# Backward value products on block-diagonal weights, new instruction orders, and other queues in the last stage

## The chip, the cores and the metric

One NeuronCore of a Trainium2 chip runs the whole program as one launch. Its five instruction streams are TensorE (PE in the profile; PEld is its weight loads), VectorE (DVE), ScalarE (ACT), GpSimd (POOL) and SyncE (SP), which only issues transfers; ScalarE and GpSimd issue transfers too. The metric is the device time of the launch in microseconds. Before the change six runs gave 3076.02 to 3081.55 us, median 3080.12 us.

## What is computed

The program computes the output and all ten gradients of `x + A(layernorm(x)) + B(layernorm(x))`. B is an MLP with a squared ReLU (512 to 1792 to 512). A is an attention over 64 segments of 32 rows, with 32 heads of 128 and 8 memory rows which each segment takes from the output of the one before, so the segments run one after the other:

```python
for s in range(n_seg):                       # 64
    xs = x[:, s * seg_len:(s + 1) * seg_len, :].copy()   # 32 rows
    h = jnp.concatenate([mem, xs], axis=1)   # 8 + 32 rows
    q = jnp.einsum('btd,dhe->bhte', h, Wq)
    k = jnp.einsum('btd,dhe->bhte', h, Wk)
    v = jnp.einsum('btd,dhe->bhte', h, Wv)
    scores = jnp.einsum('bhqe,bhke->bhqk', q, k) * scale
    scores = jnp.where(mask[None, None], scores, -1000000000.0)
    p = _softmax(scores, axis=-1)
    o = jnp.einsum('bhqk,bhke->bhqe', p, v)
    o = jnp.einsum('bhte,hed->btd', o, Wo)
    mem = o[:, :M, :].copy()
    outs.append(o[:, M:, :])
```

Inputs and outputs are bf16; the sequence has 2048 rows of width 512. The backward goes through the segments from the last to the first. In it, the gradient of v is the product of the transposed softmax weights with the gradient of the attention's output (the "value product"), one 32x128 head at a time, 32 heads a segment.

## The kernel before

*Stages*, by their place in the profiled execution: the MLP, the layernorm and first loads up to about 300 us; 64 forward steps, about 304 to 1185; the backward of left rows and the MLP's weight gradients, to 1455; 64 backward steps, 1455 to 2445; the last stage, the weight gradients of Wq, Wk, Wv, Wo and the gradient of x, to 3079.5.

*Rows and left rows.* A step's 40 rows are held as 32 that it works on in turn (8 memory rows and the segment's last 24) and the segment's first eight, its "left rows". Four steps form a block; the left rows of a block (4 x 8) are projected and have their gradients multiplied by the weights together, in operations named `L.*`. 32 heads lie as four head groups (`HG`, on 32 partitions each) of eight heads (`KH`).

*The order.* Each stage of steps is written out by hand: `F_ORDER` and `B_ORDER` are four strings each, one for each place of a step in its block, and `play` goes through the names in them and issues each operation. A `-` or `+` behind a name takes the operation from an earlier or later step (or block), so work of neighbouring steps is interleaved. The strings set the order of every engine's queue. `ENGS` says for each PSUM-to-SBUF copy whether ScalarE (helper line L372) or VectorE (L375) does it.

*A backward step* in the names of `B_ORDER`:

- `o0mm`, `o1mm` (L390): the output gradient's rows times Wo; `o*ev` copies them to `gON`; `o*fl` (L163) flips them through TensorE, and `o*te` copies the flips to `gOT`.
- `vp0`, `vp1`: the value products of heads 0-3 and 4-7 of each head group, by `outer` (L545). For each head, `outer` issues a matmul of a 32-row group: weights `gON[32g:32g+32, 128 columns]`, right side `P` (32x40), then one of the left rows (weights `b_gOL`, right side `b_PG`, 16 columns), into a PSUM round of two tiles (`b_pp`). Four head groups run on four row groups of the array. `vea`, `veb` copy heads' rows out, `vla`, `vlb` the left part (`b_gvL`).
- `s0`, `s1` (L435), `d1*` to `d4*`, `tu*`: the gradient of the scores, of which `gS` and `gST` come.
- `kp*`, `qp*`: the same kind of outer products for k and q, with evacuations `ke*`, `kl*`, `qe*`.
- `vg*`, `kg*`, `qg*` (L458): the products with Wv, Wk, Wq, gathered into one PSUM tile; `ra`, `rb` copy it, `ta`, `tb` (L467) transpose it, `HT` and `xt` (L480) reduce over the head groups. `HT` hands the 8 memory rows to the step that follows.
- `ldp`, `ldq`, `ldn` (L1216 to L1219) load P, q and k rows of a step, on GpSimd's queue; `ldk` and `vtr` use SyncE's. `vc` (L1229, L1230) builds `b_vT` on GpSimd from the transposed v rows (`b_vl`) and from `b_vTL`, the left rows, which `ldt` loads by a DMA transpose, once a block.
- For a block, `L.tr`-operations (`qtr`, `ktr`, `vtr`, L1171) transpose the left gradients by DMA into `gNat`, `*st` (L1173) store them, `L.xt` sums the left rows into the first 8 columns of `b_XT`, and `L.sx` stores it to `S_XG`. `ldv` loads `b_PG` and `b_gOL`.

*The last stage* (`slot_side`, `rows_of`, `loads`, `input_rows`, `leave`, and the loop that follows): sixteen columns of weight gradients, each eight products of 20 matmuls of 128x512. `slot_side` loads the two sides, `GOc` (of `S_GM`) and `HNc` (of `S_HT`), by 16 DMA transposes of 512 columns and four plain loads each, on SyncE's queue. `rows_of` loads the other side of each column, `gn`: for Wo by plain loads (the first column's on ScalarE's queue, others on SyncE's), for the others by 16 DMA transposes (L1387). Three buffers of it turn, and column i issues the load for i + 2. The first column's eight products run row block by row block at once, over eight PSUM tiles; each later column runs one product after the other. `leave` copies a product to `wt` on ScalarE (L1437) and stores it from the same queue (L1438). `input_rows` makes the gradient of x for one block of rows after each column (TensorE transposes at L1418, the rest on VectorE, ScalarE and GpSimd, its transfers on GpSimd's queue).

Of the kernel before, what the change touches and what calls it, by code (L numbers as in the profile page):

```python
# [26 lines left out]
def kernel(  # L27
# [114 lines left out]
    S_XG = dram.tile([NB, P, DC, P], F32, name="S_XG")  # L142

# [327 lines left out]
    def left_sums(XT, T):  # L471

        for c in range(DC):
            nc.vector.tensor_reduce(XT[:, c, :, 0:M], T[:, c * P:(c + 1) * P].rearrange("p (g j t) -> p j t g", g=HG, j=SPB),
                                    axis=AX.X, op=ALU.add)
# [103 lines left out]
    def play(order, n, steps, lefts, step, blk, done=None):  # L579
# [22 lines left out]
        "L.oa0 HT",  # L602
        "k0mm xt- q1mm k0ev q1ev q0mm L.oa1 q0ev k1mm L.out- q0fl k0fl q1fl k1ev L.mst- k1fl q0Te kl k0Te k1Te s0 "
        "q1Te L.X0 s1 mx0 sb0 mx1 v0mm km v1mm ex0 L.ob1 v0ev L.lq+ sb1 su0 rc0 L.sx- L.ldL+ ex1 pm0 v1ev tu0 "
        "w0 L.P2 su1 rc1 pm1 tu1 w1 oa0 soV- ld ob0 g0 L.otr oa1 ob1 g1 rb L.P3 ra tb L.E3 ta HT",
        "q0mm k1mm L.E2 k0mm q0ev k1ev k0ev q1mm kl k0fl soP- xt- q0fl L.mtr k1fl q1ev ld L.lo k0Te q1fl q0Te "
        "q1Te s0 L.hl++ L.t3 k1Te mx0 s1 sb0 v0mm ex0 mx1 su0 sb1 rc0 pm0 v0ev tu0 ex1 su1 v1mm rc1 pm1 w0 tu1 "
        "v1ev L.X1 L.G1 ob0 w1 oa0 oa1 ob1 g0 g1 rb L.lb ra L.P5 soN L.E5 tb ta L.G0 HT",
        "q0mm L.ra q1mm k0mm k1mm xt- q1ev soV-- q0ev k0ev L.u3 k1ev q0fl k0fl q0Te q1fl L.lp km- L.ta kl "
        "k1fl soN-- k0Te q1Te L.tb s0 k1Te s1 v0mm mx0 sb0 L.t2 soP- mx1 sb1 ex0 v1mm ex1 su0 rc0 km soV- v0ev "  # L610
        "pm0 tu0 L.S0+ kl+ su1 w0 v1ev L.P4 L.u2 rc1 pm1 tu1 w1 oa0 ob0 g0 L.xt oa1 L.mx0+ L.t1 ob1 L.E4 g1 rb "
        "L.sb0+ tb ra L.ex0+ ta HT L.S1+ k1mm+ q0mm+ L.lv+ L.su0+ k0mm+ q1mm+ xt k1ev+ L.rc0+ L.mx1+ q0ev+ "
        "k0ev+ L.sb1+ L.pm0+ q0fl+ q1ev+ q0Te+ soV k0fl+ L.ex1+ k0Te+ k1fl+ k1Te+ L.X2 q1fl+ s0+ q1Te+ s1+ "
        "mx0+ L.u1 sb0+ mx1+ soP sb1+ ex0+ su0+ v1mm+ rc0+ ex1+ pm0+ v0mm+ L.t0 ld v0ev+ ld+ su1+ tu0+ L.P0+ "
        "rc1+ pm1+ L.lm+ km+ w0+ tu1+ v1ev+ L.P1+ w1+ L.hs+ L.tu0+ oa0+ L.su1+ ob0+ oa1+ L.rc1+ g0+ L.pm1+ "
        "ob1+ L.tu1+ g1+ ra+ soP+ L.u0 soN L.W0+ L.BT rb+ L.E0+ L.E1+ ta+ tb+ L.ob0+ soN+ L.W1+")
    ENGS = on_engines(
        "L.E0 L.E1 L.E3 L.E4 L.E5 L.oa1 L.ob1 k0ev k1ev oa0 ob0 ob1 q0ev q1Te q1ev rb v0ev v1ev",
        "L.E2 L.oa0 L.ob0 L.pm0 L.pm1 L.ra k0Te k1Te oa1 pm0 pm1 q0Te ra")
    with sb("fw", 1) as fw, psum("fr", 4) as fr, psum("fpp", 1) as fpp, \  # L620
# [64 lines left out]
        def left(b):  # L685
# [62 lines left out]
            o["xt"] = lambda: left_sums(B_["XT"], st["T"])  # L748
# [185 lines left out]
    with sb("la", 2) as la, sb("ls", 2) as ls, sb("lo", 1) as lo_, sb("wg", 2) as wg, psum("lpp", 1) as lpp, psum("lr", 4) as lr:  # L934
# [9 lines left out]
        def lback(i_):  # L944
# [64 lines left out]
            def so():  # L1009
                pdma(S_GOL[b], T["gON"][:])  # L1010
                pdma(S_GSL[b], T["gS"][:])
                pdma(S_GQL[b], T["gq"][:])
# [72 lines left out]
        "ldk- ldp- vp0 L.ko0 vp1 s0 L.tb- L.ldk L.xt- d10 ldn- veb o1fl d20 vea d30 L.sx- L.H0 d40 vg0 o1te ldq- s1 "  # L1085
        "vla vlb kp0 L.qo1 tu0 kla0 ldp d11 d21 qp0 qeb0 d31 d41 qea0 klb0 vtr kea0 vg1 tu1 qg0 kp1 qp1 keb1 keb0 "
        "kla1 qeb1 L.ktr kea1 kg0 ldn qea1 kg1 vtr+ qg1 ra L.G1 ldq rb L.ra0 tb ta HT",
        "L.H1 o0mm o0ev o1mm o1ev ldk- vp0 o0fl klb1- xt- vp1 vc- vea o0te veb L.I1 s0 ldp ldn o1fl L.kst vg1 d10 vlb "
        "d20 d30 o1te d40 tu0 vla s1 kp0 L.vtr d11 qp0 kea0 keb0 d21 qea0 ldq ldk L.vst vg0 qeb0 d31 kla0 d41 klb0 "
        "tu1 kg0 qp1 kp1 keb1 qg0 kea1 kg1 vc qea1 qeb1 qg1 rb L.I2 vtr+ klb1 tb ra ta HT",  # L1090
        "L.H2 o0mm o1mm xt- o0ev kla1- o1ev o0fl vp0 vp1 o0te s0 L.G2 vea vc L.qtr L.ra1 veb L.I3 d10 o1fl d20 d30 "
        "vlb d40 vg0 o1te s1 tu0 d11 d21 qp0 qeb0 vla d31 kp0 qea0 d41 tu1 vg1 qg0 kla0 klb0 kea0 L.ra2 L.qst qp1 "
        "vtr+ kp1 keb0 qea1 L.gl+ kla1 keb1 kea1 qeb1 kg0 kg1 klb1 ldk qg1 rb L.G3 L.ldt+ tb ra ta L.H3 HT",
        "ldp- o0mm o1mm L.gs+ o0ev L.ra3 vp0 o0fl o1ev o0te vp1 s0 vea o1fl xt- veb o1te vla d10 d20 vlb d30 d40 ldq- "
        "tu0 ldn- vg1 s1 kp0 qp0 keb0 kea0 d11 qeb0 L.ldv+ vg0 klb0 d21 qea0 kg0 d31 kla0 d41 tu1 kp1 kea1 qp1 qea1 "
        "L.lq+ qeb1 klb1 keb1 vc qg0 L.vo1+ qg1 kg1 L.I0+ rb kla1 ra tb L.vo0+ ta HT L.G0+ o0mm+ xt o0ev+ o1mm+ o0fl+ "
        "L.qo0+ L.ta o0te+ o1ev+ L.ko1+")
    ENGS = on_engines(
        "L.ra0 kea0 kea1 keb0 kla0 klb0 o0ev o1ev o1te qea0 qea1 rb vea veb vla vlb",
        "keb1 kla1 klb1 o0te qeb0 qeb1 ra")  # L1100
    with sb("bq", 1) as bq, sb("bt", 1) as bt, sb("bs", 2) as bs, sb("be", 1) as be, psum("bpp", 1) as bpp, psum("br", 4) as br:
        G4 = {n: bq.tile([P, HG, KH, SPB, SEG], BF16, name="g" + n) for n in "vkq"}
        gS = bq.tile([P, KH, KW], BF16, name="gS")
        nc.vector.memset(gS[:], 0.0)

# [8 lines left out]
        def block(b):  # L1114
            if b not in blk:
                shapes = {"gkL": (bs, [P, KH, HG, NL], BF16), "gvL": (bs, [P, KH, HG, NL], BF16),
                          "gqL": (bt, [P, KH, HG, NL], BF16), "PG": (be, [P, 1, KH, KW], BF16), "GL": (be, [P, 1, KH, KW], BF16),
                          "gOL": (be, [P, GW], BF16), "qNL": (be, [P, GW], BF16), "vTL": (bs, [P, KH, HG, NL], BF16),
                          "XT": (bs, [P, DC, SPB, SEG], F32), "R4": (bt, [P, D], F32)}

                def make(n):
                    pool, shape, dt = shapes[n]
                    return pool.tile(shape, dt, name="b_" + n, tag=n)
                blk[b] = Tiles(make)
            return blk[b]

        def left(b):
# [38 lines left out]
            o["xt"] = lambda: left_sums(B_["XT"], st["T"])  # L1166
# [21 lines left out]
        def ldv(b, q=pdma):  # L1188
            q(block(b)["PG"][:, 0], S_PL[b])
# [6 lines left out]
        def ldt(b):  # L1196
            turned_rows(block(b)["vTL"][:], b, 2)
        loads.update(gl=gl, ldv=ldv, ldk=ldk, ldt=ldt)

        def bwd(s):  # L1200
# [10 lines left out]
            def tile_of(n, shape):  # L1211
                C[n] = be.tile(shape, BF16, name="b_" + n, tag=n)
# [4 lines left out]
            o["ldp"] = ldp  # L1217
            o["ldq"] = lambda q=pdma: q(tile_of("qN", [P, GW])[:], rows[:, GW:2 * GW])
# [17 lines left out]
            for p in range(2):  # L1236
# [23 lines left out]
                def pair(i, k):  # L1260

                    return B_["PG" if i == 0 else "GL"][:, 0, k, :].rearrange("p (a n) -> p a n", a=2)[:, :, lc]

                def vp(p=p):
                    outer(pp("v"), p, ((KW, L, False, 32, T["gON"], lambda k: C["P"][:, k, 0:L]),
                                       (KW, KW, True, 32, B_["gOL"], lambda k: pair(0, k))), p * 4 * KW)

                def kp(p=p):
                    outer(pp(p), p, ((KW, L, False, 32, C["qN"], lambda k: gS[:, k, 0:L]),
                                     (KW, KW, True, 32, B_["qNL"], lambda k: pair(1, k))))  # L1270
# [4 lines left out]
                o["vp%d" % p], o["kp%d" % p], o["qp%d" % p] = vp, kp, qp  # L1275
                for t, n in ((2, "v"), (1, "k"), (0, "q")):
                    for x, h in enumerate("ab"):
                        gs = slice(2 * x, 2 * x + 2)
# [224 lines left out]
```

## Time and profile before

| | |
|---|---|
| median of six runs | 3080.12 us (3076.02 to 3081.55) |
| the profiled execution | 3081.3 us; its span in the trace 3079.5 us |
| granted TensorE clock, mean | 0.965 |
| TensorE matmuls | 2693.3 us busy (87%), 51523 instructions |
| TensorE weight loads | 1396.7 us (45%), 51672 instructions |
| VectorE | 1241.6 us (40%) |
| ScalarE | 1052.4 us (34%) |
| GpSimd | 421.1 us (14%) |
| instruction fetch queue (q8) | 405 packets, 6.64 MB |
| backward vp, first matmul form at L545 (windows 1471 to 2424) | 1984 matmuls, 178 ns each from start to end |
| backward step, mean by place in the block | 13.89, 14.83, 16.21, 16.62 us |
| forward step, mean | 13.65 us |

A step's time here is the distance from one `HT` reduce (L480 on VectorE) to the next. Four matmuls on the four row groups run at once, so a matmul's own 178 ns tell less than the distance between the first instructions of two operations. Busy time of PEld overlaps PE.

### The profile page before, as it was taken

What the parts mean: (1) busy time and instruction counts of PE and PEld (TensorE: products, weight loads), DVE (VectorE), ACT (ScalarE), POOL (GpSimd) and SP (SyncE); (2) the same over time, 40 slices, a digit from 0 to 9 for tenths busy, and PEclk for the clock granted to TensorE, in tenths of its full rate; (3) what the DMA queues carried; (4) which work ended last, traced back from release to release, by engine and by line L of the source; (5) the groups of instructions that cost most, each with busy time, mean ns of one, the idle gap of its engine ahead of it and who ended that gap; (6) DMA issues with size and microseconds to landing.
All of it is one profiled execution on the core that took longest, in us unless ns stands there. A gap on an engine that the chain in (4) does not pass through costs nothing.

```text
span 3079.5 us, 115221 instructions
## 1 busy us (share of the span) xinstructions
PE 2693.3 (87%) x51523; PEld 1396.7 (45%) x51672; DVE 1241.6 (40%) x3479; ACT 1052.4 (34%) x2392; POOL 421.1 (14%) x769
## 2 busy tenths in 40 slices
PE   7996899999999886887888889888888659999998
PEld 3453444454544444456444444444444324444444
DVE  5452556556555554333444444444444300100011
ACT  2422445545554444333333333333333201111111
POOL 0000000000000000112222122212221101111111
PEclk9998999999999998999999999999999879999999
DMA  9648376767767667976578667766776689999991
GB/s 245 195 135 258 97 181 176 188 165 181 182 176 177 152 164 191 231 226 197 139 170 192 169 165 178 191 161 165 171 185 173 212 179 203 243 206 208 207 203 45
DMA packets 819442, 560.84 MB, mean 182 GB/s; under 512 B 595281, under 2 KB 711778, under 8 KB 815618
## 3 DMA queue, kind: packets, MB, share of 16 engines
q1 hardware_dynamic: 767618, 436.24, 60.3%
q0 software_dynamic: 28576, 94.01, 10.1%
q10 hardware_dynamic: 22752, 23.21, 2.7%
q8 instruction: 405, 6.64, 0.9%
q14 instruction: 91, 0.75, 0.1%
HBM read 188.36 MB, written 233.32 MB: 137 GB/s over the span
## 4 chain that ended last, share of the span: by engine, by line
PE 37%; issue 5%; ACT 4%; DVE 3%; SPq 2%; DMA 1%; POOL 0%; ACTq 0%; POOLq 0%; DVEq 0%
PE ps_gw L1464 14%; PE ps_gR L458 10%; PE b_pp L545 4%; PE ps_proj L390 4%; PE ps_RL L1156 2%; PE ps_sum L467 2%; SPq L1372 1%; ACT gk L372 1%; ACT gON L372 1%; ACT gv L372 1%; ACT R L372 1%; PE ps_sc L435 1%; DVE gq L375 1%; PE ps_tr L163 1%; SPq L1387 0%
## 5 line engine op out<-in xcount | busy, mean ns | idle before, releaser
L1464 PE MATMUL ps_gw<-gn,HNc 128*128 128x512 bf16 x1884 | 414.5, 379 | 1.9
L1464 PEld LDWEIGHTS <-HNc 128*128 128x128 bf16 x1920 | 187.9, 98 | 223.8
L372 ACT CAST f_N<-ps_proj 128x512 bf16<-128x512 f32 x384 | 218.4, 586 | 193.2 <-PE ps_proj L390 177.4
L1437 ACT CAST wt<-ps_gw 128x512 bf16<-128x512 f32 x128 | 74.4, 585 | 523.2 <-PE ps_gw L1464 257.7
L390 PEld LDWEIGHTS <-X 128*32 128x32 bf16 x6144 | 156.7, 97 | 164.3 <-DVE X L480 13.9
L1420 DVE TENSOR_TENSOR gx<-ps_rows,gb 128x512 f32<-128x512 f32 x16 | 11.1, 692 | 511.7 <-PE ps_rows L1418 511.7
L1464 PE MATMUL ps_gw<-GOc,gn 128*128 128x512 bf16 x625 | 141.5, 385 | 63.0 <-DMA GOc<-S_GM 42.9
L458 PE MATMUL ps_gR<-Wv,gv 128*32 128x512 bf16 x2048 | 148.7, 383 | 9.6 <-ACT gOT L372 4.2
L458 PE MATMUL ps_gR<-Wk,gk 128*32 128x512 bf16 x2048 | 145.8, 404 | 11.3 <-ACT gk L372 5.8
L458 PE MATMUL ps_gR<-Wq,gq 128*32 128x512 bf16 x2048 | 141.0, 399 | 4.5 <-issue 4.5
L390 PE MATMUL ps_proj<-Wk,X 128*32 128x512 bf16 x2048 | 130.0, 383 | 7.4 <-DVE X L909 5.4
L832 POOL COPY kM<-f_kT 128x256 bf16<-128x256 bf16 x64 | 25.6, 401 | 802.4 <-DVE f_kT L375 802.4
L390 PE MATMUL ps_proj<-Wq,X 128*32 128x512 bf16 x2048 | 128.7, 381 | 6.5 <-DVE X L480 6.5
L372 ACT CAST gON<-ps_proj 128x512 bf16<-128x512 f32 x128 | 74.8, 585 | 166.0 <-PE ps_proj L390 166.0
L458 PE MATMUL ps_R<-Wo,OT 128*32 128x512 bf16 x2048 | 127.5, 392 | 0.7 <-ACT Wk L372 0.7
L390 PE MATMUL ps_proj<-Wo,GT 128*32 128x512 bf16 x2048 | 123.9, 384 | 4.4 <-POOL GT L1186 3.3
L467 PE MATMUL ps_sum<-identF,R 128*128 128x128 f32 x512 | 100.0, 294 | 31.6 <-ACT R L372 24.3
L1464 PEld LDWEIGHTS <-gn 128*128 128x128 bf16 x640 | 63.4, 99 | 139.8 <-issue 67.3
L390 PE MATMUL ps_proj<-Wv,X 128*32 128x512 bf16 x2048 | 121.6, 378 | 0.0
L372 ACT CAST gk<-b_pp 128x256 bf16<-128x256 f32 x192 | 65.9, 382 | 139.8 <-PE b_pp L545 133.0
L467 PEld LDWEIGHTS ps_sum<-identF,R 128*128 128x128 f32 x512 | 54.6, 142 | 102.7 <-ACT R L372 76.7
L375 DVE COPY R<-ps_gR 128x256 f32<-128x256 f32 x64 | 27.2, 425 | 162.5 <-ACT R L372 120.6
(250 smaller groups left out, 4899.5 us busy)
## 6 DMA issues: line engine op xcount, KB each, us to landing
S_A<-f_N SPq DMA_DIRECT2D x64, 512.0 KB
S_A<-f_N SPq DMA_DIRECT2D x64, 256.0 KB
S_GB<-gv SPq DMA_DIRECT2D x32, 512.0 KB
S_GB<-gq SPq DMA_DIRECT2D x32, 512.0 KB
S_GB<-gk SPq DMA_DIRECT2D x32, 512.0 KB
out_dram<-wt ACTq DMA_DIRECT2D x128, 128.0 KB
b_kN<-S_A POOLq DMA_DIRECT2D x63, 256.0 KB, 4.0
b_qN<-S_A POOLq DMA_DIRECT2D x63, 256.0 KB, 4.1
```

What stands on the lines that cost most here:

```text
L163: nc.tensor.transpose(ps_ap, in_ap, ident[base:base + k, base:base + k])
L372: nc.scalar.copy(out, in_)
L375: nc.vector.tensor_copy(out, in_)
L390: nc.tensor.matmul(o, lhsT=hT[:, dc, :], rhs=x, start=(dc == 0), stop=(dc == DC - 1), tile_position=(0, 32 * g))
L435: nc.tensor.matmul(sc3[32 * g:32 * g + 32, k, c:c + n], lhsT=qT[:, 4 * h + k, g, :], rhs=kT[:, 4 * h + k, g, :], start=(mask is None), sto ...
L458: nc.tensor.matmul(o, lhsT=XT(k, g), rhs=x, start=(first and k == 4 * h), stop=(last and k == 4 * h + 3), tile_position=(0, 32 * g))
L467: nc.tensor.transpose(st["T"][:, c * P:(c + 1) * P], R4()[:, c * P:(c + 1) * P], identF[:])
L545: nc.tensor.matmul(o, lhsT=N_[32 * g:32 * g + m, kk * P:(kk + 1) * P], rhs=X(kk)[32 * g:32 * g + m], start=(i == 0), stop=(i == len(jobs) ...
L1156: nc.tensor.matmul(ps["R", i][32 * g:32 * g + 32, :].rearrange("p (a b) -> p a b", b=P), lhsT=B_[n][:, k, g, :], rhs=W(g * KH + k), start= ...
L1372: nc.sync.dma_start_transpose(t_[:, b:b + 4, dc * P:(dc + 1) * P], srcT[:, dc, b * P:(b + 4) * P])
L1437: nc.scalar.copy(wt[:], ps[:])
L1464: nc.tensor.matmul(ps[:], lhsT=l(rc), rhs=r(rc), start=(n == 0), stop=(n == RC_ALL - 1))
```

## The change

*Value products.* P goes from its load tile to `PD`, a tile in which each head group's 40 columns lie beside those of the others, each on its own 32 partitions, and all else is zero (GpSimd memsets both such tiles once). The copy is a new operation `pb` of four GpSimd copies a step. The left rows' P is loaded straight into its counterpart `PGD`, by four transfers a block. Per head number, one matmul with the full 128x128 weights `gON` then makes the products of all four head groups (160 columns), and a second one with `gOL` adds the left part (64 columns). A half's results lie in one PSUM tile, so its two copies need that half alone. `P` has two buffers.

```diff
+        PD = be.tile([P, HG, KH, L], BF16, name="PD")
+        PGD = be.tile([P, HG, KH, KW], BF16, name="PGD")
...
+            for g in range(HG):
+                q(PGD[32 * g:32 * g + 32, g], S_PL[b][32 * g:32 * g + 32])
...
+            def pb():
+                for g in range(HG):
+                    nc.gpsimd.tensor_copy(PD[32 * g:32 * g + 32, g], C["P"][32 * g:32 * g + 32, :, 0:L])
...
                 def vp(p=p):
-                    outer(pp("v"), p, ((KW, L, False, 32, T["gON"], lambda k: C["P"][:, k, 0:L]),
-                                       (KW, KW, True, 32, B_["gOL"], lambda k: pair(0, k))), p * 4 * KW)
+                    for k in range(4 * p, 4 * p + 4):
+                        o = pp("v")[p][:, k % 4 // 2, k % 2 * 256:k % 2 * 256 + 256].rearrange("p (g n) -> p g n", g=HG)
+                        nc.tensor.matmul(o[:, :, 0:L], lhsT=T["gON"][:, k * P:(k + 1) * P], rhs=PD[:, :, k, :],
+                                         start=True, stop=False, skip_group_check=True)
+                        nc.tensor.matmul(o.rearrange("p g (a n) -> p g a n", a=2)[:, :, :, 0:M],
+                                         lhsT=B_["gOL"][:, k * P:(k + 1) * P],
+                                         rhs=PGD[:, :, k, :].rearrange("p g (a n) -> p g a n", a=2)[:, :, :, lc],
+                                         start=False, stop=True, skip_group_check=True)
```

*Left rows.* The transposed left rows of v are stored to `S_VTL` by the left backward stage and loaded from there without a transpose (one buffer instead of two). `b_XT` has one buffer, its first columns are set to zero on GpSimd, and the left sums go to a tile of their own, `b_XL`, stored by the new `L.sl`; the last stage copies them in.

```diff
         def ldt(b):
-            turned_rows(block(b)["vTL"][:], b, 2)
+            dma(block(b)["vTL"][:], S_VTL[b])
...
+                st["XL"] = bt.tile([P, DC, SPB, M], F32, name="b_XL", tag="XL")
+                left_sums(st["XL"], st["T"])
...
+            o["sl"] = lambda: dma(S_XGL[b], st["XL"][:])
...
+                if j == SPB - 1:
+                    nc.gpsimd.memset(B_["XT"][:, :, :, 0:M], 0.0)
```

*Orders.* All eight strings are new, and some copies change engines: in the forward q0ev goes to VectorE and the left operations L.E0, L.E3, L.oa1, L.ob1 and L.E2, L.oa0, L.ob0 change sides; in the backward keb1 and kla1 go to ScalarE, o1te, kea1, klb0 and qea1 to VectorE. As an example, the first of the backward strings begins:

```diff
-        "ldk- ldp- vp0 L.ko0 vp1 s0 L.tb- L.ldk L.xt- d10 ldn- veb o1fl d20 vea d30 L.sx- L.H0 d40 vg0 o1te ldq- s1 "
+        "L.H2 L.ktr L.gl+ klb1- o0mm o1mm kla1- L.ra1 vc- o0ev o0fl xt- o0te vp0 s0 d10 o1ev vla vea d20 vp1 o1fl vg0 "
```

*Last stage.* The sides go through ScalarE's queue, in four transposes of all 2048 rows each; the first two columns' rows and all stores of `leave` go through GpSimd's. One tile (`gap5`) only shifts the address of `GOc`.

```diff
         def slot_side(t_, srcT, src):
-            for b in range(NB - 4, -1, -4):
-                for dc in range(DC):
-                    nc.sync.dma_start_transpose(t_[:, b:b + 4, dc * P:(dc + 1) * P], srcT[:, dc, b * P:(b + 4) * P])
+            for dc in range(DC):
+                nc.scalar.dma_start_transpose(t_[:, 0:NB, dc * P:(dc + 1) * P], srcT[:, dc, :])
...
-                dma(t_[:, NB + c, :], lv[c][:, 0:M, :])
+                nc.scalar.dma_start(t_[:, NB + c, :], lv[c][:, 0:M, :])
...
-            q = nc.scalar.dma_start if i == 0 else dma
+            q = pdma if i < 2 else dma
...
+            XL = p5.tile([P, DC, SPB, M], F32, name="XL5", tag="XL5")
+            pdma(XL[:], S_XGL[b])
+            nc.vector.tensor_copy(XT[:].rearrange("p c (j r) -> p c j r", j=SPB)[:, :, :, 0:M], XL[:])
...
-            nc.scalar.dma_start(dst, wt[:])
+            pdma(dst, wt[:])
```

## The prediction, made before the changed kernel ran

> **What bounds the kernel now.** I read the windows view first, one row per stage. Columns: stretch, length, busy time of each engine with its instruction count, granted clock, DMA share, GB/s.
>
> ```profile
> core 0: us, PE busy (x) PEld busy (x) DVE busy (x) ACT busy (x) POOL busy (x), PEclk, DMA share, GB/s
> 300.00:1185.00 885.00, 807.67 (x18627) 427.38 (x18683) 505.46 (x1540) 432.18 (x953) 57.24 (x154) 0.99 0.65 166
> 1455.00:2445.00 990.00, 861.65 (x24900) 441.89 (x24900) 450.15 (x1329) 354.77 (x976) 221.59 (x379) 0.98 0.70 171
> 2445.00:2488.00 43.00, 0.58 (x1) 0.28 (x3) 0.55 (x1) 0.00 (x0) 4.24 (x8) 0.51 1.05 314
> 2560.00:3040.00 480.00, 477.68 (x2210) 221.35 (x2252) 47.05 (x70) 69.59 (x138) 69.04 (x95) 1.00 1.00 199
> ```
>
> The forward steps (row 1), the backward steps (row 2) and the main run of the last stage (row 4) are all TensorE's: no other engine is busy for much over half. Row 3 is different: 43 us in which TensorE does one matmul. So the last stage can only win at its start, and the steps only through TensorE's own work and its gaps. Next, the waits of the backward steps (windows 1471 to 2424; total us, count, longest):
>
> ```profile
> PEld L545 <- issue: 106.8, 166, 2.9
> ...
> PE b_pp L545 <- issue: 35.8, 28, 2.8
> ACT gv L372 <- PE b_pp L545: 35.2, 61, 2.1
> ```
>
> "issue" means that no semaphore held the engine: TensorE's own stream was late. All of it worth naming is at L545, the outer products vp, kp, qp, which are the densest instructions. One such place in the chain of waits:
>
> ```profile
> 2305.72 2.53 issue
> 2308.25 0.29 PE b_pp L545 x17
> 2308.53 4.40 PE ps_gR L458 x48
> ```
>
> 2.53 us with nothing to wait for, in the middle of a qp, and then 48 gathers that take 4.40 us where such a run elsewhere takes 2.73: the clock granted after the gap is about half for some 3.4 us. I find 20 gaps over 1 us in the backward, 38.4 us together, nearly all in kp or qp, and 12 such slow stretches (41 us, so 20 us lost): 58 us by direct count. A second count: steps by their place in a block of four take 13.89, 14.83, 16.21, 16.62 us on the mean (61.56 a block), and the fastest of each place 56.21; 16 blocks by 5.35 is 86 us. I take the middle, 72 us, as the price of late instructions. The queue that fetches instructions moved 405 packets of 16 KB; TensorE ran 51523 + 51672 instructions, so one packet per 255, three for a step of 781.
>
> Last stage, TensorE's timeline (start, length, what, idle before and its releaser):
>
> ```profile
> 2487.34 0.58 PE L1464 MATMUL ps_gw<-GOc,gn 128*128 128x512 bf16 x1 [42.86 <-DMA GOc<-S_GM]
> ...
> 2547.44 12.84 PE L1464 MATMUL ps_gw<-GOc,gn 128*128 128x512 bf16 x48 [19.20 <-ACT wt L1437]
> ```
>
> The first gap ends with the side GOc, the second with ScalarE freeing PSUM; ScalarE itself was late because its stores sat behind SyncE's row of transposes:
>
> ```profile
> 2546.80 1.07 ACT L1437 CAST wt<-ps_gw 128x512 bf16<-128x512 f32 x2 [23.68 <-DMA gn<-S_GB]
> ```
>
> **The change, part by part**, against the profiled execution's 3081.3 us (span 3079.5).
>
> *Value products.* Each half of vp was 32 matmuls on row groups, 40 or 16 columns wide, four at once. From the first to the next operation behind it:
>
> ```profile
> 2425.45 0.20 PE L545 MATMUL b_pp<-b_P,gON 32*128 32x40 bf16 x4
> ...
> 2425.75 0.40 PE L163 MATMUL ps_tr<-ident,gON 128*128 128x128 bf16 x4
> ```
>
> that is 0.30 us. After: 8 full matmuls, four of 160 columns and four of 64, with weights 128x128. Row 4 above gives 477.68/2210 = 216 ns for 512 columns, so 0.42 ns a column: 68 and 27 ns. The 128-column flips at L163, also with full weights, follow each other at 60 ns, so the 64-column ones cost 27 (columns) to 60 (weights). A half is 4x68 + 4x27..60 = 0.38 to 0.51, plus one uncovered weight load, 98 ns in the last stage's row of L1464: 0.48 to 0.61, so 0.18 to 0.31 more; by 128 halves 23 to 40 us. Part may fall into the idle 1.4 us of a step (TensorE is occupied 830 of 952 us here; 38 of the other 123 are the gaps above), so the low end is 0. I take +30, nearer the rows since vp is mostly followed by other TensorE work. The Trainium skill, TensorEngine Tiling (Array Packing), section Theoretical Speedup, gives up to 4x for contractions of 32 or less run on four row groups, which speaks against this part. Here half of vp in 0.30 us against my 0.48 to 0.61 gives 1.6 to 2x; by the page's 4x the part would be +115 us (128 x 0.9), which the column price doesn't bear out.
>
> *Fewer instructions.* 32 matmuls and 32 weight loads per half become 8 and 8: 96 fewer per step, 781 to 685 as built. What matters is whether the fetch keeps up. Laying the built orders out at the trace's pace, the share of places where over 240 instructions fall into 3 us is 25.6% before and 13.1% after, and the mean excess there drops to about 0.4 of its own. The vp instructions sit just ahead of the kp/qp runs that stall, so I take 0.58 of the 72 us: -42 (bounds: 0, since the stalls lie in kp and qp, which stay as they are, and -86). The Trainium skill, Runtime: NRT & Kernel Launch, section Instruction fetch mechanics, calls the price of crossing a 16 KiB block mostly hidden; by it this term would be 0. The trace shows 2.5 us where it isn't.
>
> *Block-diagonal copies.* pb adds 4 GpSimd copies a step (32x320 elements). The nearest row:
>
> ```profile
> L1230 POOL COPY b_vT<-b_vTL 128x256 bf16<-128x256 bf16 x62 | 25.2, 407 | 0.0
> ```
>
> Four at 0.41 to 0.5 are 1.6 to 2 us a step, 103 to 128 us on GpSimd, which is busy 222 of 990: cover enough, at nothing. But pb waits for the vp of the step before (one PD) and stands in GpSimd's queue before the loads (ldp, ldq, ldn, each 0.54 us of issue and 3.7 to 4.1 to land) and vc, and the next vp1 stands before s0 or vea on TensorE; if late, see the last rival. P has two buffers, so its own load has a step of room. The four diagonal loads of S_PL replace one per block (3 more issues x 0.54 x 16 = 26 us of GpSimd, hidden alike). The transposed load of vTL becomes a plain one: 16 transposes fewer on SyncE, which doesn't bound a step; at nothing. XT single, XL and its store (a SyncE issue of 0.3 us): at nothing, hidden by the block's 60 us; XT's GpSimd memset waits for S_XG's store of the block before, and without cover delays pb by the store's 4 us.
>
> *Orders.* Backward: vea and vla now need only vp0, and the row above shows ScalarE waiting 35.2 us for vp; 85 us of dependence idle are left on TensorE. I take -6, a fourteenth (bounds -20 to +15: the new order could as well open waits). Forward: 52 of 720 us idle on TensorE; one more left-row operation covers the wait for the R copy; -6 (bounds -15 to +10). The moved copies (q0ev, L.E*, keb1, kea1, o1te) trade 382 ns on ScalarE for 420 on VectorE, both half idle: nothing.
>
> *Last stage.* The gap follows SyncE's queue:
>
> ```profile
> 2453.50 2.94 SPq L1171 DMA_TRANSPOSE gNat<-b_gvL  x1
> ...
> 2475.95 23.26 SPq L1372 DMA_TRANSPOSE GOc<-S_GM  x16
> ```
>
> GOc's transposes begin 33 us after the steps' end (2442.5), behind the left rows' (gNat) and their stores. After: GOc is on ScalarE's queue in 4 transposes of 512 KB; each takes 5.2 us uncongested, by one of that size in the trace. But as built, each transpose on one queue waits for the landing of the one before on the other, so GOc's alternate with gNat and the gn rows on SyncE, and the first matmul needs all four. Walked by hand, the first matmul comes 50 to 57 us after the steps' end (44.8 before). Then the second gap: stores leave on GpSimd (128 x 0.54 us, 69 us of a queue busy 69 of 480), ScalarE waits no more for SyncE, and 19.2 becomes 0 to 7. Sum: -6 (bounds -20, both gaps at their best, to +15, one more round of 512 KB transposes at the congested 8 to 9 us). The Trainium skill, DMA: Bandwidth & Descriptors, section on two transposing streams in flight at once, demands exactly that the later stream waits for the earlier's full landing; no trace here shows what happens otherwise, and it speaks against sides on a second queue. XL's copy and load per column: 0.5 us on VectorE busy a tenth: nothing.
>
> *Ends.* Memsets and pb ahead of the first vp, about +3; the tail's last stores on a software queue, +1.
>
> Sum: 3081.3 + 30 - 42 - 6 - 6 - 6 + 4 = 3055.3; the profiled execution stands 1.2 above the median of six, so 3054.
>
> **The rivals.**
> - *All stalls go* (0.20): the excess falls below what the fetch makes good. For it: the gaps are 20 of 64 steps, so the fetch just fails. Against: kp and qp stay. -72, orders -12 and -10, last stage -10, +30 +4: 3011, less 1.2: 3010.
> - *The stalls stay* (0.15; slower): they lie in kp/qp, which keep 64 + 64 instructions a half at the same pace; vp's 32 fewer come too early to help. Price: only 10 of 72 us go, no order gain: +30 - 10 - 6 - 6 + 4 = +12, 3092. It decides once fewer than 22 us of the 72 go.
> - *The last stage loses* (0.12): transposes alternate over two queues at the congested 8 to 9 us, +20 instead of -6: 3080, no change.
> - *pb late* (0.08; slower): vp0 waits for PD and s0, vea wait behind it; 1 us a step, 64 us: 3118. Against: GpSimd is busy under a quarter.
>
> **How the numbers follow.** The forecast has 0.45, alone 3035 to 3075. About 0.2% (6 us) can't be told from no change. Range 2998 to 3098: left out are pb late and thin ends of the first two rivals. Faster: 0.41 of the forecast, 0.20 and 0.03 of the last-stage case, 0.64; same: 0.03 + 0.03 + 0.06 = 0.12; slower: 0.01 + 0.12 + 0.03 + 0.08 = 0.24.
>
> **What would show it.** Backward block mean 61.56 to about 59 us; issue waits at L545 above 1 us from 38 to 15 us or less; vp half 0.48 to 0.61; GpSimd about 335 of 990; first ps_gw 50 to 57 us after the steps, no second gap; forward step 13.65 to 13.55. It is wrong if the stalls keep their count, if vp0 shows a wait for PD, or if a vp half takes over 0.7.

## The result, and the profile after

The change made the kernel slower: 3093.94 us median of 18 runs (3084.42 to 3101.76) against 3081.29 us of the kernel before (39 runs, 3070.62 to 3094.07). The ratio is 1.004, 95% interval 1.0029 to 1.0051. The profiled execution took 3088.5 us (span 3086.7).

The windows view of the kernel after, in the columns shown before (the stage between the backward and the main run is cut at its own first matmuls):

```profile
core 0: us, PE busy (x) PEld busy (x) DVE busy (x) ACT busy (x) POOL busy (x), PEclk, DMA share, GB/s
300.00:1185.00 885.00, 810.77 (x18655) 419.70 (x18711) 567.88 (x1632) 388.01 (x869) 56.00 (x149) 0.99 0.66 168
1455.00:2445.00 990.00, 854.90 (x21860) 442.59 (x21860) 481.10 (x1398) 322.32 (x916) 371.02 (x713) 0.98 0.74 176
2445.00:2490.00 45.00, 0.00 (x0) 0.00 (x0) 0.00 (x0) 0.00 (x0) 3.72 (x6) 0.50 0.90 243
2490.00:2560.00 70.00, 46.64 (x207) 21.27 (x213) 3.64 (x6) 5.49 (x12) 10.08 (x18) 0.81 0.80 165
2560.00:3040.00 480.00, 477.74 (x2210) 221.41 (x2252) 46.64 (x81) 69.51 (x136) 138.12 (x225) 1.00 0.98 201
```

The backward has 3000 matmuls fewer, and the main run of the last stage is unchanged. The stretch without TensorE has grown, as the timeline of TensorE shows:

```profile
2435.20 0.66 PE L469 MATMUL ps_sum<-identF,b_R 128*128 128x128 f32 x4 [0.80 <-DVE b_R L1174]
2512.93 0.59 PE L1503 MATMUL ps_gw<-GOc,gn 128*128 128x512 bf16 x1 [76.64 <-DMA GOc<-S_GM]
```

The backward ends 8 us earlier than before, but the first weight-gradient matmul comes 26 us later: 76.6 us idle, where it was 42.9 and then 19.2 us. Stage by stage, between the same events in both traces:

| profiled execution, us | before | after | difference |
|---|---|---|---|
| start to the first forward reduce | 320.0 | 318.0 | -2.0 |
| forward, first to last reduce | 846.3 | 844.5 | -1.8 |
| last forward reduce to the end of the left backward's outer products | 285.8 | 294.2 | +8.4 |
| from there to the first backward reduce | 19.0 | 25.0 | +6.0 |
| backward, first to last reduce | 952.2 | 933.1 | -19.1 |
| last reduce to the last matmul of the backward | 21.2 | 21.5 | +0.3 |
| from there to the first weight-gradient matmul | 42.9 | 76.6 | +33.7 |
| from there to the end | 592.2 | 573.7 | -18.5 |

The differences sum to +7. The medians differ by 12.7. Of the missing 5 to 6 us the profiles show a likely place: seven profiles with this same backward (the kernel after and six variants below) took 931 to 945 us in it, median 939, so the profiled execution of the kernel after was some 6 us short there.

What holds the first weight-gradient matmul is in SyncE's timeline of the kernel after:

```profile
2432.86 1.82 SPq L1187 DMA_TRANSPOSE gNat<-b_gkL  x1
2434.73 1.15 SPq L1182 DMA_DIRECT2D S_XGL<-b_XL  x1
2435.98 13.63 SPq L1422 DMA_TRANSPOSE gn<-S_GB  x2
2449.70 0.54 SPq L1189 DMA_DIRECT2D S_GL<-gNat  x1
2450.28 20.77 SPq L1422 DMA_TRANSPOSE gn<-S_GB  x2
2471.15 1.25 SPq L1187 DMA_TRANSPOSE gNat<-b_gvL  x1
```

L1422 loads the third column's rows, which TensorE first reads at 2584.6, 149 us after the first of these transposes. (The last stage's queues are not ordered by hand as those of the steps are: in the code the sides stand ahead of the third column's rows, in the built program these come first.) Four of these transposes stand ahead of the left rows' (gNat), and they take 34 us to issue while GpSimd's loads of two columns fill the transfers (311 GB/s from 2436 to 2478, DMA share 1.04, by the windows view). The transfers were as full in the first gap of the kernel before (314 GB/s, share 1.05); new is what stands in SyncE's queue there. Only at 2478 does ScalarE's queue start on GOc, and then the chain of waits goes back and forth:

```profile
2478.26 4.58 DMA GOc<-S_GM
...
2484.14 3.92 DMA gn<-S_GB
...
2488.14 4.58 DMA GOc<-S_GM
...
2494.07 4.06 DMA gn<-S_GB
...
2498.20 4.55 DMA GOc<-S_GM
...
2502.77 4.08 DMA gn<-S_GB
...
2506.87 5.82 DMA GOc<-S_GM
```

Each GOc transpose waits for the landing of a transpose on SyncE's queue and the other way round. From 2478 to 2513 only 138 GB/s move.

### The profile page after: what moved, and what is told of

Its sections match the earlier page's. It is cut to its first block, busy times and chain, and to the rows that moved or that the text cites. A ratio compares the mean times of both kernels' runs of the same rounds, so it can differ in the third digit from the quotient of the medians.

```text
span 3086.7 us, 109583 instructions
## 1 busy us (share of the span) xinstructions
PE 2684.3 (87%) x48451; PEld 1387.5 (45%) x48600; DVE 1332.3 (43%) x3645; ACT 972.4 (32%) x2242; POOL 657.3 (21%) x1264
## 5 line engine op out<-in xcount | busy, mean ns | idle before, releaser
L374 ACT CAST f_N<-ps_proj 128x512 bf16<-128x512 f32 x320 | 185.9, 581 | 244.1 <-PE ps_proj L392 225.8
L1503 PE MATMUL ps_gw<-GOc,gn 128*128 128x512 bf16 x625 | 139.6, 382 | 77.6 <-DMA GOc<-S_GM 76.6
L460 PE MATMUL ps_gR<-Wq,gq 128*32 128x512 bf16 x2048 | 148.3, 392 | 14.4 <-DVE gq L377 6.6
L392 PE MATMUL ps_proj<-Wk,X 128*32 128x512 bf16 x2048 | 134.9, 384 | 12.7 <-DVE X L482 6.9
L460 PE MATMUL ps_gR<-Wv,gv 128*32 128x512 bf16 x2048 | 135.8, 385 | 0.5 <-issue 0.5
L469 PE MATMUL ps_sum<-identF,R 128*128 128x128 f32 x512 | 92.6, 291 | 39.6 <-ACT R L374 35.7
L1238 POOL COPY PD<-b_P 32x320 bf16<-32x320 bf16 x256 | 114.9, 449 | 56.8 <-DMA b_P<-S_A 48.9
L1476 POOL DMA_DIRECT2D out_dram<-wt x128 | 69.2, 542 | 263.3 <-ACT wt L1475 259.8
L1251 POOL COPY b_vT<-b_vl 128x1024 bf16<-128x1024 bf16 x64 | 66.4, 1038 | 253.9 <-PE ps_sc L437 190.6
```

What stands on the lines that cost most here:

```text
L374: nc.scalar.copy(out, in_)
L392: nc.tensor.matmul(o, lhsT=hT[:, dc, :], rhs=x, start=(dc == 0), stop=(dc == DC - 1), tile_position=(0, 32 * g))
L460: nc.tensor.matmul(o, lhsT=XT(k, g), rhs=x, start=(first and k == 4 * h), stop=(last and k == 4 * h + 3), tile_position=(0, 32 * g))
L469: nc.tensor.transpose(st["T"][:, c * P:(c + 1) * P], R4()[:, c * P:(c + 1) * P], identF[:])
L1238: nc.gpsimd.tensor_copy(PD[32 * g:32 * g + 32, g], C["P"][32 * g:32 * g + 32, :, 0:L])
L1251: nc.gpsimd.tensor_copy(vT[:, :, :, 0:SEG], C["vl"][:])
```

## The experiments

Times are medians; every ratio is to the kernel before, on the same chip. "First gap" is TensorE's idle time between the backward and the first weight-gradient matmul.

**1. The last stage's queues of before, in the changed kernel** (`e1_old_last`).

```diff
-            for dc in range(DC):
-                nc.scalar.dma_start_transpose(t_[:, 0:NB, dc * P:(dc + 1) * P], srcT[:, dc, :])
+            for b in range(NB - 4, -1, -4):
+                for dc in range(DC):
+                    nc.sync.dma_start_transpose(t_[:, b:b + 4, dc * P:(dc + 1) * P], srcT[:, dc, b * P:(b + 4) * P])
...
-                nc.scalar.dma_start(t_[:, NB + c, :], lv[c][:, 0:M, :])
+                dma(t_[:, NB + c, :], lv[c][:, 0:M, :])
...
-            q = pdma if i < 2 else dma
+            q = nc.scalar.dma_start if i == 0 else dma
...
-            pdma(dst, wt[:])
+            nc.scalar.dma_start(dst, wt[:])
```

> The changed kernel with the last stage's queues as before (sides in 16 transposes on SyncE, rows of the first two columns on ScalarE and SyncE, stores on ScalarE). In the changed kernel TensorE stands still for 76.4 us between the backward and the first weight-gradient matmul; before it was 42.9 us, and a second gap of 19.2 us followed. Theory (the last stage's queues are what lost): both gaps come back, 62 us together, the time falls by 14 us to about 3080, ratio to the kernel before 0.9995. Rival (the loss lies in the middle of the program and in the backward's own drain): the first gap stays above 60 us, and the ratio stays at 1.004 or rises with the second gap.

Measured: 3061.1 us, ratio 0.9931 (0.9910 to 0.9952), against 1.004 with the new queues: about 33 us. TensorE's timeline of this kernel:

```profile
2471.78 15.81 PE L1504 MATMUL ps_gw<-GOc,gn 128*128 128x512 bf16 x64 [26.10 <-DMA GOc<-S_GM]
2489.84 20.88 PE L1504 MATMUL ps_gw<-GOc,gn 128*128 128x512 bf16 x96 [2.26 <-DMA GOc<-S_GM]
2529.46 32.39 PE L1504 MATMUL ps_gw<-GOc,gn 128*128 128x512 bf16 x140 [13.98 <-ACT wt L1476]
```

The queues are what lost, and by more than expected: the two gaps that were to come back with 43 and 19 us come back with 26.1 and 14.0. GOc's first four transposes now stand ahead of gNat's last one on SyncE, where the kernel before had all of GOc behind it. SyncE's timelines, of this kernel and then of the kernel before:

```profile
2465.00 5.17 SPq L1408 DMA_TRANSPOSE GOc<-S_GM  x4
2470.27 1.25 SPq L1187 DMA_TRANSPOSE gNat<-b_gqL  x1
```

```profile
2466.72 1.24 SPq L1171 DMA_TRANSPOSE gNat<-b_gqL  x1
```

So the rest of the change is a gain that the new queues more than ate. This kernel beats both.

**2. Only the sides back on SyncE** (`e2_sides_sp`: the first two pieces of the diff above).

> The changed kernel with only the two sides back on SyncE in 16 transposes; first rows and stores stay on GpSimd. Theory A (transposes alternate over two queues, each waiting for the other's landing): the first gap falls from 76 to about 45 us, no second gap over 5 us, the time falls by 30 us, ratio about 0.995. Theory B (the rows of two columns, loaded at once by GpSimd, crowd the transfers, so the transposes of the left gradients take 11 to 17 us each): the gap stays above 65 us, ratio 1.001 to 1.004.

Measured: 3079.29 us, ratio 0.9991 (0.9974 to 1.0007), first gap 47.2 us, then another gap of 10 us at the first `input_rows`, which neither theory has. Theory A holds for the first gap, but the time gains only half of it. Against experiment 1, 21 us of first gap are left, so A is not the whole.

**3. Only the first two columns' rows back** (`e3_rows_back`: the third piece).

> The changed kernel with only the rows of the first two columns back on their queues (ScalarE for the first, SyncE for the second); sides stay on ScalarE, stores on GpSimd. Theory A (alternating transposes): the gap stays near 70 us, ratio 1.002 to 1.004. Theory B (crowding by two columns' rows at once): the first GOc transpose starts 15 to 20 us earlier, gap 50 to 60 us, ratio 0.997 to 0.999.

Measured: 3091.61 us, ratio 1.0041 (1.0026 to 1.0056), first gap 64.0 us and a second of 10.3 us. The first gap lies between the two theories, the time is A's. TensorE's first weight-gradient matmul in this kernel:

```profile
2495.26 37.50 PE L1503 MATMUL ps_gw<-GOc,gn 128*128 128x512 bf16 x160 [64.04 <-DMA GOc<-S_GM]
```

No transpose of the third column stands ahead of GOc here (SyncE's first comes at 2485.1). ScalarE's four GOc transposes begin at 2461.0, behind the first column's rows on the same queue, and take 34 us up to this matmul, as long as in the changed kernel. With the sides on ScalarE, the rows' queue hardly matters for the time (3092 against 3094 us); with the sides on SyncE (experiment 2 against experiment 8) it is worth 21 us. The two edits overlap: against experiment 8 the rows alone lose 21 us, the sides alone 33 and both 35.

**4. The left rows of v transposed again** (`e4_vtl_back`).

```diff
-                pdma(S_VTL[b], T["vTL"][:])
...
-            dma(block(b)["vTL"][:], S_VTL[b])
+            turned_rows(block(b)["vTL"][:], b, 2)
```

> The changed kernel with the left rows of v transposed again in the backward instead of stored by the left backward and loaded plainly. In the left backward stage of the changed kernel TensorE waits 12.9 us for wB (2.6 before), and SyncE's transpose of l_vTL starts 6 us after the load ahead of it. Theory (the store of l_vTL holds its buffer, so SyncE's next transpose and the wA and wB loads behind it are late): that wait falls to 2 to 4 us, the time by 9 us, ratio about 1.001. Rival (the load is late because TensorE comes earlier, the store has nothing to do with it): the wait stays at 9 to 13 us and the ratio at 1.004.

SyncE in the left backward, of the kernel after and then of the kernel before:

```profile
1318.56 0.37 SPq L958 DMA_DIRECT2D l_vTM<-S_VTM  x1
1324.87 2.39 SPq L556 DMA_TRANSPOSE l_vTL<-S_NL  x1
...
1331.73 5.01 SPq L1031 DMA_DIRECT2D wB<-S_GH1N  x1
```

```profile
1317.85 0.32 SPq L955 DMA_DIRECT2D l_vTM<-S_VTM  x1
1318.27 1.26 SPq L554 DMA_TRANSPOSE l_vTL<-S_NL  x1
```

Measured: the wait for wB falls from 12.9 to 4.2 us, just above the theory's 2 to 4, and the stretch to the end of the left backward from 294.2 to 283.0 us. The other profiles agree on the direction: in all four without this store (the kernel before and experiments 4, 5 and 6) the wait is 2.6 to 4.2 us and the stretch 282.7 to 286.6 us; in the nine that have it and the loads' order of the changed kernel the wait is 8.2 to 12.9 us and the stretch 286.5 to 295.0 us. By the means of the two groups the store costs some 6 us, so the +8.4 of the table is a high sample. But the time doesn't follow: 3097.06 us, ratio 1.0049 (1.0033 to 1.0065). The first backward step took 21.1 us instead of 18.3 in this profile (TensorE waits 2.7 us for `b_qNL` there), and the backward 939.7 us. So the store does hold SyncE up, and undoing it with its transposes gains nothing measurable.

**5. Only the stores moved, in the kernel before** (`e5_stores_pool`: `pdma(dst, wt[:])` in `leave`).

> The kernel before with only the stores of the last stage's products moved from ScalarE to GpSimd. Theory (the 19.2 us gap after the first column is ScalarE's copies queued behind its own blocked stores): that gap falls below 5 us, the time by 15 us, ratio 0.995. Rival (the stores were only the place where the wait showed; TensorE then waits for the side HNc or for rows that SyncE brings just as late): a gap of 12 us or more stays, with another releaser, ratio 0.998 to 1.000.

Measured: 3067.37 us, ratio 0.9962 (0.9943 to 0.9980). The first gap is 45.4 us, the 19.2 us gap is gone; the largest gap behind it is 5.3 us. This part of the change was worth 12 us by itself.

**6. All three queue changes, in the kernel before** (`e6_new_last`).

> The kernel before with all three queue changes of the last stage (sides on ScalarE in 4 transposes, first rows and stores on GpSimd), all else as before. Theory (these queues lose by themselves): the first gap grows from 42.9 us to 75 us or more, the second goes, ratio 1.004 to 1.007. Rival (they lose only together with the new backward order, which leaves the left rows' transposes elsewhere): first gap 50 to 57 us, ratio 0.997 to 1.000.

Measured: 3108.21 us, ratio 1.0087 (1.0069 to 1.0106), 27 us slower and beyond the theory's range, with no second gap and this first one:

```profile
2531.96 0.58 PE L1463 MATMUL ps_gw<-GOc,gn 128*128 128x512 bf16 x1 [93.76 <-DMA GOc<-S_GM]
```

The queues lose by themselves; no new order is needed for it.

**7. The old value products in the new order** (`e7_old_vp`).

```diff
-                    for k in range(4 * p, 4 * p + 4):
...
+                    outer(pp("v"), p, ((KW, L, False, 32, T["gON"], lambda k: C["P"][:, k, 0:L]),
+                                       (KW, KW, True, 32, B_["gOL"], lambda k: pgair(k))), p * 4 * KW)
...
-         vp0 s0 d10 o1ev vla vea d20 vp1 o1fl vg0
+         vp0 s0 d10 o1ev d20 vp1 vea veb vla o1fl vg0
```

> The changed kernel with the value products on row groups as before (32 matmuls a half, P and PG read directly, no PD, no pb); the orders stay, but for the copies of v, which now stand behind the second half. The backward from first to last step took 933 us in the changed kernel (931 to 941 in its variants) and 952 before, with issue gaps over 0.9 us of 14 to 19 us and 39 us. Theory (the forecast's: full matmuls cost some 25 us of TensorE, fewer instructions save more): a vp half returns from 0.50 to 0.30 us, issue gaps return to 30 us or more, the backward takes 945 to 960 us. Rival (the new order is what shortened the steps, the value products only cost): gaps stay at 14 to 19 us and the backward takes 905 to 915 us.

Measured: 3143.51 us, ratio 1.0198 (1.0175 to 1.0222). Issue gaps over 0.9 us are back at 38 us in 21 places, as the theory has it, but the backward takes 999.5 us, far above its 945 to 960: all TensorE idle time in it rose from 112 to 150 us, and gathers now wait 17.8 us for copies of v that had to be moved. It shows that the gaps return with the instructions; it doesn't price the value products.

**8. Sides and rows as before, stores on GpSimd** (`e8_stores_only`).

> The changed kernel with sides and first rows on the queues of before; only the stores of the last stage stay on GpSimd. With the stores on ScalarE too, this order ran at 0.9931 of the kernel before, with a first gap of 26 us and a second of 14 us that ended with ScalarE's copies. Theory (copies behind blocked stores make the second gap): it falls below 4 us, ratio 0.988 to 0.990. Rival (the side HNc, late on SyncE, makes it): it stays at 10 us or more with HNc or the rows named, ratio 0.992 to 0.994.

Measured: 3058.64 us, ratio 0.9930 (0.9907 to 0.9953), no better than experiment 1 within the intervals; the ratio is the rival's. The 14 us gap is gone; in its place stand five waits of 1.3 to 4.7 us for the third column's rows, 11 us together. The copies made the gap, but SyncE's transposes would have made it next.

**9. Two repairs more, on experiment 8's kernel** (`e9_best`; the diff shows these two alone).

```diff
+                chunk(i_ + 1)
                 if i_ + 1 < NB:
                     load(i_ + 1)
-                chunk(i_ + 1)
...
-        nc.gpsimd.memset(PD[:], 0.0)
-        nc.gpsimd.memset(PGD[:], 0.0)
+        nc.vector.memset(PD[:], 0.0)
+        nc.vector.memset(PGD[:], 0.0)
```

> The changed kernel with sides and first rows on the queues of before and stores on GpSimd (ratio 0.993 so far), and two edits more: the left backward issues the loads of wA and wB ahead of the five loads of the next block, and PD and PGD are set to zero by VectorE instead of GpSimd. Theory (the 12.9 us wait for wB comes from SyncE's order, and the 6.7 us wait for GT from GpSimd's 3.0 us of memsets in front of GT's own): the waits fall to 4 to 7 us and to 3.5 us, the first backward step from 18.3 to 16 us; 8 to 12 us in all, ratio 0.989 to 0.991. Rival (the wB load is late because the transfers are full, and GT's wait ends with another operation): the waits stay within 2 us of what they were, ratio 0.993.

Measured: 3063.36 us, ratio 0.9941 (0.9921 to 0.9962), no faster than experiment 8. GT's wait falls from 6.7 to 3.9 us and the first step from 18.3 to 16.7. The wait for wB goes, but TensorE then stands 6.9 and 3.6 us for l_vTM and l_vTL, which come after it on SyncE. So the memsets are priced (some 4 us, too little to see in the time), and the loads were only put in another order.

**10. The new value products in the old order** (`e10_old_order`: `B_ORDER` and the engines of before, with `pb`, `L.sl` and `L.sx` put in and `ldp` a step earlier; last stage as before). The pieces of strings are shown against the kernel before.

```diff
-         "ldk- ldp- vp0 L.ko0 vp1 s0
+         "ldk- vp0 L.ko0 vp1 s0
...
-         vtr kea0 vg1 tu1 qg0 kp1 qp1 keb1 keb0 kla1 qeb1 L.ktr kea1 kg0 ldn qea1
+         vtr kea0 vg1 tu1 qg0 kp1 qp1 keb1 keb0 kla1 qeb1 L.ktr kea1 kg0 ldn pb qea1
```

> The changed kernel with the backward's order and engines of the kernel before (pb and the store of the left sums put in, P loaded a step earlier, S_XG stored at the end of its block) and the last stage's queues of before: what the new value products do in the old order. The backward took 952 us before and 931 to 941 in the changed kernel's variants. Theory (fewer instructions relieve the fetch; the order adds little): issue gaps over 0.9 us fall from 39 us to 15 to 20, the backward takes 935 to 945 us. Rival (the new order is what shortened it; in the old one the value products only add their 0.2 us a half): gaps stay above 30 us, the backward takes 960 us or more.

Measured: 3068.1 us, ratio 0.9961 (0.9946 to 0.9976). The backward takes 945.7 us (952.2 before), the issue gaps over 0.9 us fall from 39.4 us in 21 places to 16.5 in 10, inside the theory's range (with the waits for other engines of that length 23 us); the backward lies just above its 935 to 945. The first gap is 29.9 us, so most of this kernel's gain is not in the backward. Against the median of 939 us in the new order, order and value products would be worth some 6 us each. But this is one profile, and the seven profiles of the new order's backward spread over 13 us, so neither number is shown.

**11. The four large transposes on SyncE** (`e13_sides_sp4`: `nc.scalar` becomes `nc.sync` in `slot_side`).

> The changed kernel with the sides on SyncE, but in the 4 transposes of 2048 rows that the change made of the 16; first rows and stores on GpSimd. With the 16 on SyncE the first gap was 47 us and the time 3079 us, with the 4 on ScalarE 76.6 us and 3094 us. Theory (the second queue costs, since each transpose waits for the landing of the one on the other queue): gap 45 to 55 us, time 3077 to 3083, ratio 0.999 to 1.000. Rival (the size costs: no matmul can start before all four have landed): gap 65 us or more, ratio 1.002 to 1.005.

Measured: 3083.06 us, ratio 0.9994 (0.9976 to 1.0013), first gap 64.7 us. The time is at the theory's edge, the gap a hair below the rival's 65. Both act: against the changed kernel (76.6 us, 3094 us) the second queue costs 12 us of gap and 11 of time, and against experiment 2 (47.2 us, 3079 us) the size 17.5 us of gap, most of which a shorter second part gives back. From the first GOc transpose to the first matmul it takes 24 us here (2487.5 to 2511.8) and 7 us with the sixteen small ones of experiment 2 (2489.7 to 2496.7): the matmul needs all four large ones, and of the small ones the first four.

**12. Only the first column's rows on GpSimd** (`e14_rows_pool`: sides as before, `q = pdma if i == 0 else dma`).

> The changed kernel with sides as before, stores on GpSimd, and only the first column's rows on GpSimd; the second column's stay on SyncE. With both columns on their queues of before the first gap was 26.7 us (3059 us), with both on GpSimd 47.2 us (3079 us). Theory (the second column's rows on SyncE had kept the third column's transposes behind those of GOc; taken off, seven of these go first): gap 25 to 32 us, ratio 0.992 to 0.995. Rival (the rows are slower or crowd the transfers when GpSimd issues them): gap 40 us or more, ratio 0.997 to 1.000.

Measured: 3062.67 us, ratio 0.9940 (0.9917 to 0.9964), first gap 26.6 us. SyncE's timeline of this kernel:

```profile
2448.11 0.39 SPq L1420 DMA_DIRECT2D gn<-S_ON  x1
2452.39 0.33 SPq L1189 DMA_DIRECT2D S_GL<-gNat  x1
2452.77 0.43 SPq L1420 DMA_DIRECT2D gn<-S_ON  x1
2455.74 1.23 SPq L1187 DMA_TRANSPOSE gNat<-b_gvL  x1
2457.03 0.59 SPq L1420 DMA_DIRECT2D gn<-S_ON  x1
2459.32 0.33 SPq L1189 DMA_DIRECT2D S_GL<-gNat  x1
2459.95 5.19 SPq L1408 DMA_TRANSPOSE GOc<-S_GM  x4
```

Where the kernel after has the third column's transposes, this one has cheap issues of the second column's rows (L1420), and GOc begins 24 us after S_XG's store (2435.74), where experiment 2 needs 45 us (2445.05 to 2489.68). The theory holds: it is the second column's rows, not the first's, that should have stayed on SyncE.

## Why the prediction was wrong, point by point

**The step that failed** is the last stage: "Walked by hand, the first matmul comes 50 to 57 us after the steps' end", with the sum of -6 (bounds -20 to +15). Measured: 76.6 us after the last matmul of the backward (42.9 before by this count, 44.8 by the forecast's), and +15.5 us for the whole stage. The second half of that step was right: the 19.2 us gap went. GOc's own price was right: its four transposes landed in 4.6, 4.6, 4.6 and 5.8 us (forecast 5.2 each). What the walk had too short is the time on SyncE ahead of them and between them: four third-column transposes stood before GOc while two columns' rows filled the transfers, and took 34 us to issue, so GOc began 42 us after the backward's end; then the turns with SyncE took another 35 us. The prediction's last stage doesn't name the rows' move to GpSimd at all, so it didn't ask what SyncE would do in the time that the move freed. With the sides on SyncE, experiments 8, 12 and 2 show it: 3059, 3063 and 3079 us as neither, one and both columns leave. The sides then cost the rest (experiments 2, 11 and the changed kernel: 3079, 3083, 3094 us). Taken in the other order the shares differ: the sides alone cost 33 us (experiment 8 against 3, 3059 to 3092 us) and the rows another 2, so each edit spoils the start by itself and the 35 us have no single split. The rule of the Trainium skill that the prediction weighed (DMA: Bandwidth & Descriptors, two transposing streams) is kept by the built kernel: the chain above shows each side waiting for the other's landing, 4 to 6 us a turn.

**The second miss** is "The transposed load of vTL becomes a plain one ... at nothing" and "Ends ... about +3". The store that feeds the plain load holds l_vTL's buffer, and SyncE's queue waits 6 us for it with the loads of wA and wB behind: +8.4 us in the left backward, which the prediction left out (experiment 4: 294.2 back to 283.0 us; some 6 us over all profiles). The stretch with the memsets was +6.0 instead of +3: GT's memset waits behind them on GpSimd (3.3 to 6.7 us), and the first step is 2.6 us longer, with SyncE's load of PGD waiting for them too. Moving them to VectorE took 4.5 of the 6 us back (experiment 9).

**The value products** were priced right. A half in the kernel after, from TensorE's timeline:

```profile
2417.24 0.23 PE L1289 MATMUL b_pp<-PD,gON 128*128 128x160 bf16 x1
2417.31 0.19 PE L1291 MATMUL b_pp<-PGD,b_gOL 128*128 128x64 bf16 x1
...
2417.76 0.40 PE L165 MATMUL ps_tr<-ident,gON 128*128 128x128 bf16 x4
```

0.52 us to the next operation, and 0.49 for the second half (forecast 0.48 to 0.61); over all 128 halves of the trace the median is 0.49, where it was 0.30, so about +24 us for the forecast's +30. The starts are 70 and 30 ns apart, so the 64 columns have their low price. A half takes 1.6 to 1.7 times the old one. The Trainium skill's up to 4 for row groups (TensorEngine Tiling (Array Packing), Theoretical Speedup) is not reached in these narrow matmuls.

**The stalls** went as forecast. The waits of the kernel after between the first and the last backward reduce:

```profile
PE b_pp L547 <- issue: 11.1, 17, 1.5
...
ACT gv L374 <- PE b_pp L1291: 8.9, 31, 0.4
```

against 35.8 us in 28 waits before for the first. Issue gaps over 0.9 us fell from 39.4 us in 21 places to 11.4 in 8 (7 to 11 us in the variants of the same backward); "to 15 us or less" was the forecast. (With the waits for other engines of that length it is 14.0 us in 10 places, 14 to 19 in the variants; the expectation of experiment 7 calls this count issue gaps.) That these stalls are waits for instructions, which the prediction took for granted, the packets of the instruction queue (q8) in the traces show: each of the 21 before and of the 8 after ends 1.2 to 1.7 us after a packet of that queue has landed, where a moment picked at random in the backward lies so in one case of ten. The term of -42 itself isn't shown, for TensorE's idle time in the backward fell only from 123 to 112 us: its issue gaps over 0.15 us went from 51.6 to 20.2, its waits for VectorE and ScalarE rose from 57.0 to 82.5. **The orders.** The backward's -6 is not shown: ScalarE's wait for the value products fell, as the second line has it (35.2 before), but TensorE's waits for both copying engines rose, and what the new order is worth stays open (experiment 10). The forward gave -1.8 instead of -6, and that isn't clear of the spread: 841.7 to 846.3 us in three profiles of the old forward, 841.5 to 845.9 in eleven of the new. Together the backward gave -19 in the profile and -13 by the median of seven, against -18 forecast, so the sum of its terms came out near, and not each term. A block of four steps took 60.4 us (forecast about 59), and GpSimd was busy 371 us of 990 (forecast 335).

**The rivals.** The time landed beside that of "the stalls stay" (3092) by luck: the stalls went. "The last stage loses" named the place and the queues; its price, +20 for -6, was near the measured +15.5, but not by its reason alone: the alternating transposes landed in 3.8 to 5.8 us and not in 8 to 9, and half of the gap lay before the first of them. Its 3080 lacked the left backward. "pb late" is excluded: TensorE waits 0.4 us in all for PD, over 496 matmuls, and a copy takes 449 ns.

## What to carry to other kernels

When loads are moved off a queue, walk through what that queue does instead: with the work in front gone, a greedy order fills it with transfers needed much later, and these then stand ahead of the one that is needed first. Price a transfer at the start of a stage by what stands ahead of it on its queue and by how full the transfers are there. A plain load in place of a transposed one has a price on the side that writes it: follow the buffer that the new store holds to the queue that waits for it.

## What the hardware showed that was not expected

DMA transposes of gn (128x8x128 each) landed in 3.8 to 4.1 us in turn with GOc's, and two of them took 14 to 21 us to issue while plain loads of 2 KB rows ran and 311 GB/s moved in all. Alternating transposes on two queues moved 138 GB/s with 4 to 6 us a turn. And on TensorE full-weight matmuls of 160 and 64 columns start 70 and 30 ns apart, so changing all 128 weight rows before a 64-column matmul cost about what its columns do (27 ns at 0.42 ns a column).
